# One pass of exponentials for both channel halves, those of one table parked in DRAM, together with a retuned queue scheduler

## The chip, the cores and the metric

The kernel runs on one core of one Trainium2 chip. The metric is the device time of one execution in microseconds (us), taken as the median of several executions. The profile is one execution of the same program; its span runs from the first instruction to the last and is some 1.8 us shorter than the time of that same execution.

Engines: TensorE (PE) multiplies matrices, VectorE (DVE) works element by element, ScalarE (ACT) evaluates functions and also copies results out of PSUM (the memory that matmuls write to), SyncE (SP) issues most transfers. GpSimd (POOL) does next to nothing (0.2 us). SBUF is the on-chip memory for everything else. The profile lists the clock that was granted to TensorE; a stretch is called warm here where it is near 1 and cold where it is near 0.5.

## The reference, cut to what matters

The output is a gate between two branches over 2048 positions and 512 channels:

```python
g = sigmoid((x * gate_w).sum(-1, keepdims=True))
return g * a + (1 - g) * b
# a: a state-space convolution, with 512 channels x 128 states
P = exp(logdA[:, :, None] * l)                    # complex, logdA = dt * (A_re + i A_im)
K = einsum("dn,dnl,dn->dl", Cc, P, dB).real       # one filter of 2048 taps per channel
y = irfft(rfft(u) * rfft(K)) + u * Dskip
# b: the two tokens of highest score go through a gated MLP (512 -> 1792 -> 512); below: the MoE
```

The kernel doesn't compute `P` for 2048 lags. It makes two small complex tables per half of the channels (table 1 with 32 lags, table 2 with 21), so that each needed lag is a product of one entry of each. A table entry is `exp(real part)` times the sine or cosine of the imaginary part. A matmul of table 1 with table 2 over the 128 states then gives the filter ("kernel generation"). The convolution is a blocked transform written as matmuls: forward transform of the input, spectrum of the filter, products in the frequency domain, inverse transform.

## The kernel before: the parts that matter

Every operation is recorded with what it reads and writes and with an estimated cost. A list scheduler then fixes the order of each engine's queue before the program is built. It takes, again and again, the operation that its model can start first; priority only decides between equal starts.

```python
class Prog:
    DMA_LAT, DMA_BW, SEM = 1.9, 200.0e3, 0.06
    ...
    def schedule(self):
        ...
                    if o.tset is not None and o.tset != phases[ph[0]]:
                        continue                     # table phases are strictly in order
                    e = e0
                    if o.alt is not None:            # ScalarE or VectorE, whichever the model has done first
                        e = min(o.alt, key=lambda x: max(free[x], rt[o.idx]) + o.alt[x][1] + self.bias.get(x, 0.0))
                    st = max(free[e], rt[o.idx])
                    key = (st, -o.bl - o.prio)
        ...
            free[e] = st + c
        ...
                rt[s] = max(rt[s], o.end + (self.SEM if ops[s].eng != e or o.dma else 0.0))
```

Two helpers may go to either engine, by their costs. `EV` copies a result out of PSUM, `SCL` multiplies by a constant:

```python
        def EV(o, a, rd, wr, **k):
            ...  cost=(0.185 + n * 0.833e-3, 0.16 + n * 1.04e-3)      # (ScalarE, VectorE)
        def SCL(o, a, c, rd, wr, **k):
            ...  cost=(0.2 + n * 0.833e-3, 0.18 + n * 0.55e-3)
```

The kernel has to load another set of function tables (ACT_TABLE_LOAD, 1.28 us in the traces) whenever ScalarE goes from `Exp` to `Sin` or back, so the two are separated into phases, `tset` 0 to 5. Even phases are exponentials, odd ones are everything else:

```python
        def exps1(h, ts):                            # table 1 of half h: 32 calls, 256 wide
            for s in range(32):
                AC(TP[h][1](0, 128, s * 4, (128, 64), (1, 4)), AL(0, 128, h * HC, (4, 64), (1, 4)), ACTF.Exp, ..., scale=float(T1[s]), tset=ts)
        def exps2(h, ts): ...                        # table 2: 16 calls, 256 wide
        exps1(0, 0); exps2(0, 0)
        P.boost = 100.0; routing(); P.boost = 0.0    # the MoE and the gate
        tab1(0, (1, 1)); forward(); tab2(0, (1, 3))
        exps1(1, 2); xupd(); kgen(0)
        ...
        tab1(1, (3, 3)); exps2(1, 4); tab2(1, (5, 5))
        kspec(0); kgen(1); products(0, 0); products(0, 1)
        ...
        kspec(1); inverse(0); products(1, 0); products(1, 1); inverse(1)
```

The reason for the phases of half 1 in the middle is memory. Nearly all of SBUF is taken by buffers that share places in turn. Table 2 of half 1 lies where the generated filter of half 0 lies for a while, and its exponentials lie where table 2 of half 0 was.

## Time and profile before

| | before |
|---|---|
| median of 4 executions | 225.21 us (224.63 to 226.58) |
| span of the profile | 225.8 us |
| busy PE, DVE, ACT | 182.8, 173.1, 151.0 us |
| table loads of ScalarE | 6 |

The first lines are of the page's part 1: busy time, share of the span, number of instructions.

```profile
## 1 busy us (share of the span) xinstructions
PE 182.8 (81%) x1480; PEld 111.4 (49%) x1490; DVE 173.1 (77%) x283; ACT 151.0 (67%) x282; POOL 0.2 (0%) x4
```

No engine is full. To see why they take turns, follow ScalarE and VectorE in the timeline. The columns are start, duration, engine, source line, operation, output and input with their shapes, count, and in brackets the idle time just before with what ended it. L398 is the helper of ScalarE functions, L402 the copy helper `EV`, L406 the scaling helper `SCL`, L387 VectorE's two-input operation, L391 its operation with a constant. First ScalarE:

```profile
28.25 1.28 ACT L242 ACT_TABLE_LOAD   x1
56.97 1.28 ACT L398 ACT_TABLE_LOAD   x1
70.93 3.46 ACT L398 ACTIVATE AR<-AR 128x256 bf16<-128x256 f32 x11
74.41 1.28 ACT L242 ACT_TABLE_LOAD   x1
108.39 1.28 ACT L398 ACT_TABLE_LOAD   x1
119.96 1.28 ACT L242 ACT_TABLE_LOAD   x1
```

Between 57 and 76 us and between 108 and 121 us, ScalarE makes half 1's exponentials and can compute no sine. VectorE, in its timeline, runs dry there:

```profile
59.46 0.78 DVE L387 TENSOR_TENSOR AR<-AR 128x28 bf16<-128x28 bf16 x2
73.13 0.68 DVE L396 CAST AR<-ps 2x512 bf16<-2x512 f32 x1 [12.89 <-PE ps L691]
76.69 1.23 DVE L402 CAST AR<-ps 128x1024 bf16<-128x1024 f32 x1 [2.50 <-PE ps L715]
116.71 0.69 DVE L402 CAST AR<-ps 128x512 bf16<-128x512 f32 x1 [4.35 <-PE ps L748]
122.34 0.69 DVE L391 TENSOR_SCALAR AR<-AR 128x1024 int32<-128x1024 int32 x1 [4.01 <-ACT AR L398]
146.08 64.98 DVE L387 TENSOR_TENSOR AR<-AR 128x1024 bf16<-128x1024 bf16 x74 [1.67 <-ACT AR L398]
```

The last line is the products of both halves, 65 us without a gap. So VectorE's time falls in three pieces: up to the products (146 us), the products (65 us), the tail with the last inverse (15 us). TensorE waits too, in its timeline, for an output scaling (L852, L853 are the matmuls of that step) that stands in ScalarE's queue behind half 1's new sines:

```profile
130.55 0.61 PE L852 MATMUL ps<-AR 128*128 128x512 bf16 x1 [10.19 <-ACT AR L398]
```

### The profile page before, as it was taken

The numbers are of one execution on the slowest core, as the hardware profiler recorded it, in microseconds if no ns is written. First come the engines' busy times: TensorE is split into PE (matmuls) and PEld (weight loads), VectorE is DVE, ScalarE is ACT, GpSimd is POOL, SyncE is SP. The second block draws the span as 40 slices with busy tenths as digits, with TensorE's granted clock in tenths as the row PEclk, the third lists the DMA queues.
The fourth block names the chain that finished last, engine by engine and source line by source line (L and its number), as shares of the span: only waits on it lengthen the run. The fifth ranks groups of instructions, "written<-read, shape, count | busy, mean of one in ns | idle before, by whom it ended". The sixth has DMA issues, their size and how long they took to land.

```text
span 225.8 us, 3655 instructions
## 1 busy us (share of the span) xinstructions
PE 182.8 (81%) x1480; PEld 111.4 (49%) x1490; DVE 173.1 (77%) x283; ACT 151.0 (67%) x282; POOL 0.2 (0%) x4
## 2 busy tenths in 40 slices
PE   0366798959999999997893089998898999945993
PEld 0255343626443444455650013666655768834882
DVE  0729369998600599999823999799999999999863
ACT  3799999998689896399969995656834455205000
POOL 0000000000000000000000000000000000000000
PEclk9999589967699999999667555999969999995899
DMA  6999940100902000000284000000090000002054
GB/s 95 363 312 319 405 192 1 36 13 3 302 23 49 0 0 0 0 3 1 79 381 193 0 1 0 3 0 0 3 345 29 0 3 0 0 0 73 23 162 117
DMA packets 17633, 19.93 MB, mean 88 GB/s; under 512 B 8913, under 2 KB 15186, under 8 KB 17234
## 3 DMA queue, kind: packets, MB, share of 16 engines
q1 hardware_dynamic: 16274, 19.48, 26.0%
q10 hardware_dynamic: 1344, 0.23, 0.9%
q8 instruction: 11, 0.18, 0.3%
q14 instruction: 4, 0.03, 0.0%
HBM read 16.83 MB, written 2.10 MB: 84 GB/s over the span
## 4 chain that ended last, share of the span: by engine, by line
PE 49%; DVE 23%; ACT 21%; issue 3%; DMA 2%; SPq 1%; DVEq 0%; ACTq 0%
DVE AR L387 19%; PE ps L715 18%; ACT AR L398 12%; PE ps L776 8%; PE ps L826 7%; ACT AR L402 6%; PE ps L735 3%; DVE AR L391 3%; PE ps L853 2%; ACT AR L406 2%; PE ps L852 2%; PE ps L748 2%; DMA AR<-in_A_A_im_dram 2%; PE ps L691 1%; PE ps L680 1%
## 5 line engine op out<-in xcount | busy, mean ns | idle before, releaser
L387 DVE TENSOR_TENSOR AR<-AR 128x1024 bf16<-128x1024 bf16 (+6 forms) x182 | 136.9, 804 | 9.3 <-DMA AR<-in_A_A_re_dram 5.8
L402 ACT ACTIVATE AR<-ps 128x1024 bf16<-128x1024 f32 (+7 forms) x62 | 50.2, 827 | 33.9 <-PE ps L776 17.3
L398 ACT ACTIVATE AR<-AR 128x256 bf16<-128x256 f32 (+4 forms) x132 | 65.1, 559 | 3.3 <-DVE AR L387 1.5
L715 PE MATMUL ps<-AR 128*128 128x512 bf16 x248 | 62.9, 408 | 2.0 <-ACT AR L402 1.1
L715 PEld LDWEIGHTS ps<-AR 128*128 128x128 bf16 x256 | 26.4, 104 | 35.5 <-issue 8.6
L826 PE MATMUL ps<-AR 128*128 128x256 bf16 x256 | 30.6, 285 | 5.5 <-ACT AR L398 5.5
L776 PE MATMUL ps<-AR 128*128 128x256 bf16 x224 | 32.9, 284 | 0.7 <-ACT AR L402 0.7
L826 PEld LDWEIGHTS ps<-AR 128*128 128x128 bf16 x256 | 26.1, 102 | 9.8 <-DVE AR L387 5.7
L776 PEld LDWEIGHTS ps<-AR 128*128 128x128 bf16 x224 | 21.7, 100 | 12.0 <-issue 1.5
L398 ACT ACTIVATE AR<-ps,AR 128x512 bf16<-128x512 f32 (+1 forms) x32 | 16.6, 584 | 15.5 <-DVE AR L387 10.3
L391 DVE TENSOR_SCALAR AR<-AR 128x1024 int32<-128x1024 int32 (+5 forms) x32 | 16.0, 523 | 4.7 <-ACT AR L398 4.3
L406 ACT ACTIVATE AR<-AR 128x256 int32<-128x256 f32 x50 | 17.2, 404 | 0.8 <-DVE AR L387 0.7
L607 PE MATMUL ps<-AR 128*128 128x128 bf16 x64 | 7.5, 311 | 11.6 <-DMA AR<-in_A_u_dram 9.5
L735 PE MATMUL ps<-AR 128*128 128x84 bf16 x256 | 13.3, 214 | 3.2 <-ACT AR L402 3.2
L852 PE MATMUL ps<-AR 128*128 128x512 bf16 x14 | 7.2, 512 | 10.2 <-ACT AR L398 10.2
L735 PEld LDWEIGHTS ps<-AR 128*128 128x128 bf16 x256 | 11.8, 106 | 5.1 <-ACT AR L402 4.3
L607 PEld LDWEIGHTS ps<-AR 128*128 128x128 bf16 x64 | 6.5, 145 | 12.4 <-DMA AR<-in_A_u_dram 9.5
L396 DVE CAST AR<-ps 128x16 bf16<-128x16 f32 (+3 forms) x6 | 1.5, 256 | 13.7 <-PE ps L691 12.9
L402 DVE CAST AR<-ps 128x1024 bf16<-128x1024 f32 (+4 forms) x7 | 5.7, 837 | 7.0 <-PE ps L748 4.4
L394 DVE SCALAR_TENSOR_TENSOR AR<-ps,AR 128x256 bf16<-128x256 f32 x16 | 6.9, 478 | 3.9 <-PE ps L826 3.9
L852 PEld LDWEIGHTS ps<-AR 128*128 128x128 bf16 x16 | 1.6, 99 | 15.0 <-ACT AR L398 13.1
L853 PE MATMUL ps<-AR 2*128 2x512 bf16 x16 | 7.9, 495 | 0.7 <-DVE AR L402 0.5
(35 smaller groups left out, 66.7 us busy)
## 6 DMA issues: line engine op xcount, KB each, us to landing
AR<-c_ksp SPq DMA_DIRECT2D x1, 3584.0 KB, 11.2
AR<-in_A_u_dram SPq DMA_DIRECT2D x2, 1024.0 KB, 7.2
AR<-c_fwd SPq DMA_DIRECT2D x1, 2048.0 KB, 7.9
AR<-c_inv SPq DMA_DIRECT2D x1, 2048.0 KB, 7.7
out_dram<-AR SPq DMA_DIRECT2D x16, 128.0 KB, 2.2
AR<-in_B_w_gate_dram SPq DMA_DIRECT2D x1, 1792.0 KB, 11.1
AR<-in_B_w_up_dram SPq DMA_DIRECT2D x1, 1792.0 KB, 12.6
AR<-in_B_w_down_dram SPq DMA_DIRECT2D x1, 1792.0 KB, 7.9
```

What stands on the lines that cost most here:

```text
L387: return P.op(DVE, lambda h: h.tensor_tensor(out=o, in0=a, in1=b, op=op), rd, wr, cost=tt_cost(o, a, b), **k)
L391: return P.op(DVE, lambda h: h.tensor_scalar(out=o, in0=a, scalar1=s1, scalar2=None, op0=op0), rd, wr, cost=c, **k)
L398: return P.op(ACT, lambda h: h.activation(out=o, in_=a, func=func, scale=scale, bias=bias), rd, wr, cost=0.185 + nel(o) * 0.833e-3 + (0.09 ...
L402: return P.op((ACT, DVE), (lambda h: h.activation(out=o, in_=a, func=ACTF.Copy), lambda h: h.tensor_copy(o, a)), rd, wr, cost=(0.185 + n * ...
L406: return P.op((ACT, DVE), (lambda h: h.activation(out=o, in_=a, func=ACTF.Copy, scale=c), lambda h: h.tensor_scalar(out=o, in0=a, scalar1= ...
L607: last = h.transpose(bb(0, 128, db * 256 + t_ * 128, (1, 128)), U(0, 128, (2 * q + t_) * D + db * 128, (1, 128)), IDN(0, (1, 128)))
L715: last = h.matmul(o, w, U(0, 128, (blk * 8 + st * 2 + par) * D, (1, D)), start=(par + st == 0), stop=(par * 4 + st == 7 and blk == 0))
L735: last = hh.matmul(pb(0, 128, (g - b0) * 84, (1, 84)), TP[h][1 - part](0, 128, g * 128, (1, 128)), TQ[h][1 - part](0, 128, g * 84, (1, 84) ...
L776: last = hh.matmul(pb(0, 128, n * 256, (1, 256)), KP(0, np_, u * 2048 + tau * 128, (1, 128)), KC[h](0, np_, jg * 256, (1, 256)), start=(k ...
L826: last = hh.matmul(pb(0, 128, e * 256, (1, 256)), G(0, 128, ((par * 2 + part) * 4 + ft) * 512 + (2 * t2 + e) * 128, (1, 128)), X(0, 128, h ...
L852: h.matmul(pb(0, 128, c0, (1, D)), IDN(0, (1, 128)), U(0, 128, tb * D, (1, D)), start=True, stop=False)
L853: return h.matmul(pb(0, 128, c0, (1, D)), OHR(0, 2, tb * 128, (1, 128)), ZB(0, 2, D, (1, D)), start=False, stop=True)
```

## The change

Its stated intent: all exponentials of both halves come first, in one pass that is 512 wide, with one switch of tables. Half 1's table 2 exponentials are written to DRAM and read back when their place is free. To make room for half 1's table 1 exponentials, one MoE weight moves to the space of the input spectrum, so the forward transform now does all of block 0 before block 1. The diff also retunes the scheduler's costs and adds priorities ("boosts"). Two smaller edits are left out of the cut: the sign changes of the sine table, fixed on VectorE before, may now go to either engine (`SCL`), and the two parts of each forward group are separate operations. Its core, cut:

```diff
-    DMA_LAT, DMA_BW, SEM = 1.9, 200.0e3, 0.06
+    DMA_LAT, DMA_BW, SEM, OVER = 1.9, 300.0e3, 0.08, 0.085
-            free[e] = st + c
+            free[e] = st + c - (self.OVER if e in (ACT, DVE) and not o.dma else 0.0)
-                rt[s] = max(rt[s], o.end + (self.SEM if ops[s].eng != e or o.dma else 0.0))
+                rt[s] = max(rt[s], o.end + (self.SEM if ops[s].eng != e or o.dma else 0.03))
 # EV, the copy out of PSUM: (ScalarE, VectorE)
-                        cost=(0.185 + n * 0.833e-3, 0.16 + n * 1.04e-3), **k)
+                        cost=(0.185 + n * 0.833e-3, 0.16 + n * (1.04e-3 if a.dtype == F32 else 0.52e-3)), **k)
 # SCL
-                        cost=(0.2 + n * 0.833e-3, 0.18 + n * 0.55e-3), **k)
+                        cost=(0.19 + n * 0.833e-3, 0.165 + n * (0.48e-3 if a.dtype == F32 else 0.245e-3)), **k)
 ...                                               # and the costs of two VectorE helpers and of small matmuls
+        PK = Buf(P, "park", AR[:, :], "dram", 0, 4, BF)
+        park = nc.dram_tensor("park", (128, 4 * KB), BF).ap()
-        def exps1(h, ts):
+        def exps1(ts):
             for s in range(32):
-                AC(TP[h][1](...), AL(0, 128, h * HC, (4, 64), (1, 4)), ACTF.Exp, ...)
+                AC(two(TP[0][1], TP[1][1], s * 4, 128), AL(0, 128, 0, (HC, 2), (4, 64), (1, 4)), ACTF.Exp, ...)
 ...                                               # exps2 likewise: half 0 in place, half 1 into ST
-            for ft in range(4):
-                for blk in range(NBLK):            # forward
+            for blk in range(NBLK):
+                for ft in range(4):
-        exps1(0, 0)
-        exps2(0, 0)
+        exps1(0)
+        exps2(0)
+        DMA([(... park ..., ST(0, 128, 0, (1, 4 * KB)))], [ST], [PK], 1048576)
-        tab2(0, (1, 3))
-        exps1(1, 2)
+        P.boost = 30.0
+        tab2(0, (1, 1))
+        P.boost = -30.0
+        tab1(1, (1, 1))
+        P.boost = 0.0
         xupd()
+        P.boost = 60.0
         kgen(0)
-        tab1(1, (3, 3))
-        exps2(1, 4)
-        tab2(1, (5, 5))
+        DMA([(B("eb1b", oE, 8 * KB)(...), ... park ...)], [PK], [...], 1048576)
+        tab2(1, (1, 1))
```

## The prediction

> **What bounds it now.** No engine binds alone: busy are TensorE 182.8, VectorE 173.1, ScalarE 151.0 of 225.8 us. The chain of waits runs over TensorE (49%), VectorE (23%) and ScalarE (21%) in turn. The timeline shows three parts.
> - Up to 146 us, VectorE builds the tables of both halves. It is idle here for about 43 us: 5.8 at the start, 4.6 (25 to 30 us), 12.9 (60 to 73) and 2.5, 4.4 and 4.0 (112 to 122), the rest small.
> - From 146 to 211 us, it does the spectral products without a gap.
> - The last inverse and the output follow, about 15 us.
>
> The idle stretches at 60 to 78 and 112 to 122 are ScalarE's doing: the Sin of later tables must wait until half 1's exponentials (57 to 74, 108 to 120) are done, with a table switch on either side. TensorE waits 10.2 us there too, at 120 us, for an output scaling that stands in ScalarE's queue behind new Sin work; its matmuls then run cold (granted clock 0.54 from 120 to 139 us; 512 wide spaced 0.54 us instead of 0.22).
>
> **What it removes.** 96 exponentials 256 wide become 48 that are 512 wide. In a queue, 26 of the former took 7.94 us, 0.305 each, 29 us in all; the latter are an estimated 0.52 each, 25 us. Six table loads of 1.28 us become two. ScalarE saves about 9 us. More important, no exponential phase lies in the middle, so Sin, scalings and evictions may come in any order, and half 1's first table can fill the wait for half 0's kernel generation. The Trainium skill ("ScalarE: Activation LUTs", What ACT_TABLE_LOAD costs) gives 1283 ns for the load, as the trace, and about as much for a drain, which the trace does not show.
>
> **What it adds.** The first exponential phase grows by about 48 x 0.21 = 10 us, and with it the switch (28.2 us now) moves to about 37 to 40. Forward matmuls, routing and copies fill part of that on TensorE and VectorE. Parking writes and reads 1 MB each; from 2 MB landing in 7.7 us I estimate 4 to 6 us each. The write is off the path; the read waits for kernel generation 0 and is mostly hidden by its selection step. Six more small weight loads in the forward (5.7 us to landing, against about 7 us of matmuls each) should hide. MoE weights in spectrum space delay only the second block. The retuned scheduler costs reorder all queues: not separable in advance.
>
> **Critical path.** VectorE from 30 to 146 us has about 88 us of work. Starting it 10 us later, with routing and some copies done before, and 6 to 8 us of idle, tables end at an estimated 125 to 131. The products (65) and the tail (15) follow unchanged: 205 to 211. From TensorE: forward starts at 24 us, about 168 us of matmuls at the warm spacing and a tail of 4 give 196 without a stall, and 8 to 10 us of stalls are likely. Both meet near 207.
>
> **Predicted:** 207 us, 198 to 217 (8 in 10). Faster 0.93, same 0.05, slower 0.02.
>
> **What the profile would show.** Two table loads; 48 exponentials of about 0.62 us busy; the switch at 37 to 40 us; no VectorE gap over 6 us after 40 us; the 10.2 us TensorE wait gone and the clock there above 0.8; products starting at 125 to 133; busy sums of VectorE and TensorE within 5% of before.
>
> **What would make it wrong.** The late switch starving VectorE and TensorE for over 10 us; the parked read landing behind the 3.5 MB load (11.2 us); the small weight loads stalling the forward; half 0's kernel generation queued late behind the forward; a colder TensorE.

## The result, and the profile after

The changed kernel took 212.8 us (211.06 to 213.95, 4 executions), the kernel before in the same rounds 225.21 us. The ratio is 0.943 with a 95% interval of 0.936 to 0.951. A ratio here is the mean time of one kernel's runs over that of the other's runs of the same rounds, so it is not quite the ratio of the medians. Executions over 1.5% slower than the fastest of the same kernel are left out of the means. Later the same kernel gave 212.64 us and 0.940 (0.935 to 0.945): repeats agree to about 0.3%.

The lines that answer to those of before are of the same views. Part 1 of the page, then ScalarE and the group of exponentials, before and after (in the view of groups by shape, "25.4, 621" is busy us and mean ns of one):

```profile
## 1 busy us (share of the span) xinstructions
PE 180.4 (85%) x1490; PEld 109.8 (52%) x1490; DVE 173.8 (82%) x292; ACT 138.1 (65%) x221; POOL 0.2 (0%) x4
```

```profile
17.50 16.21 ACT L398 ACTIVATE AR<-AR 128x512 bf16<-128x512 f32 x31
33.73 1.28 ACT L242 ACT_TABLE_LOAD   x1
```

```profile
L398 ACT ACTIVATE AR<-AR 128x256 bf16<-128x256 f32 x96 | 31.0, 405 | 1.5 <-DVE AR L387 1.5
L398 ACT ACTIVATE AR<-AR 128x512 bf16<-128x512 f32 x48 | 25.4, 621 | 1.2 <-DVE AR L387 1.2
```

ScalarE saves 13 us of work. VectorE and TensorE have the same work as before. VectorE's timeline after the switch has no long hole; these are its largest ones up to the last product:

```profile
98.05 0.90 DVE L406 TENSOR_SCALAR AR<-AR 128x256 int32<-128x256 f32 x4 [1.12 <-ACT AR L398]
103.90 1.29 DVE L387 TENSOR_TENSOR AR<-AR 128x1024 bf16<-128x1024 bf16 x2 [4.95 <-DMA AR<-park]
108.20 3.10 DVE L387 TENSOR_TENSOR AR<-AR 128x1024 bf16<-128x1024 bf16 x5 [3.01 <-PE ps L773]
124.79 35.73 DVE L387 TENSOR_TENSOR AR<-AR 128x2048 bf16<-128x2048 bf16 x48 [1.82 <-ACT AR L402]
162.09 9.43 DVE L387 TENSOR_TENSOR AR<-AR 128x2048 bf16<-128x2048 bf16 x10 [1.56 <-ACT AR L402]
173.28 21.19 DVE L387 TENSOR_TENSOR AR<-AR 128x1024 bf16<-128x1024 bf16 x26 [1.76 <-ACT AR L398]
```

TensorE's wait of 10.19 us for the output scaling (its matmuls are L871 and L872 here) is gone; the longest waits there now are these:

```profile
112.63 0.39 PE L871 MATMUL ps<-AR 128*128 128x512 bf16 x1 [0.63 <-ACT AR L398]
114.15 0.61 PE L871 MATMUL ps<-AR 128*128 128x512 bf16 x1 [0.65 <-ACT AR L398]
```

Divide the two spans as VectorE's timeline divides them:

| VectorE's pieces, us | before | after | difference |
|---|---|---|---|
| up to the first product | 146.1 | 124.8 | -21.3 |
| products | 65.0 | 69.7 | +4.7 |
| after the last product | 14.7 | 16.7 | +2.0 |
| span | 225.8 | 211.2 | -14.6 |

The front became 21 us shorter, and 6.7 us of that were given back later. The product piece holds 84 VectorE instructions where it held 75: some of the last table operations of half 1 now stand among the first products, and there are two waits in it, of 1.56 and 1.76 us. So the products begin earlier than the tables end.

### The profile page after: what moved, and what is told of

Its sections match the earlier page's. It is cut to its first block, busy times and chain, and to the rows that moved or that the text cites. A ratio compares the mean times of both kernels' runs of the same rounds, so it can differ in the third digit from the quotient of the medians.

```text
span 211.2 us, 3613 instructions
## 1 busy us (share of the span) xinstructions
PE 180.4 (85%) x1490; PEld 109.8 (52%) x1490; DVE 173.8 (82%) x292; ACT 138.1 (65%) x221; POOL 0.2 (0%) x4
## 4 chain that ended last, share of the span: by engine, by line
DVE 40%; PE 32%; ACT 22%; DMA 3%; SPq 1%; issue 1%; DVEq 0%
DVE AR L387 33%; ACT AR L398 15%; PE ps L845 9%; PE ps L795 8%; ACT AR L402 5%; PE ps L767 4%; PE ps L754 3%; DVE AR L391 3%; DMA AR<-in_A_u_dram 3%; PE ps L623 2%; PE ps L734 2%; PE ps L872 1%; PE ps L871 1%; DVE AR L402 1%; DVE AR L406 1%; SPq L483 1%
## 5 line engine op out<-in xcount | busy, mean ns | idle before, releaser
L387 DVE TENSOR_TENSOR AR<-AR 128x1024 bf16<-128x1024 bf16 (+6 forms) x182 | 134.6, 798 | 19.2 <-DMA AR<-in_A_A_re_dram 5.2
L402 ACT ACTIVATE AR<-ps 128x1024 bf16<-128x1024 f32 (+7 forms) x59 | 45.5, 787 | 34.0 <-PE ps L795 19.9
L398 ACT ACTIVATE AR<-AR 128x512 bf16<-128x512 f32 (+3 forms) x84 | 59.3, 770 | 5.2 <-DVE AR L391 3.7
L734 PEld LDWEIGHTS ps<-AR 128*128 128x128 bf16 x256 | 25.6, 102 | 31.6 <-issue 5.9
L845 PEld LDWEIGHTS ps<-AR 128*128 128x128 bf16 x256 | 25.5, 101 | 9.1 <-DVE AR L387 5.2
L795 PEld LDWEIGHTS ps<-AR 128*128 128x128 bf16 x224 | 22.2, 101 | 13.6 <-ACT AR L402 2.6
L406 ACT ACTIVATE AR<-AR 128x256 int32<-128x256 f32 (+1 forms) x44 | 19.1, 492 | 0.2
L754 PEld LDWEIGHTS ps<-AR 128*128 128x128 bf16 x256 | 12.6, 110 | 7.7 <-ACT AR L402 3.7
L623 PE MATMUL ps<-AR 128*128 128x128 bf16 x64 | 6.4, 278 | 9.9 <-DMA AR<-in_A_u_dram 9.4
L391 DVE TENSOR_SCALAR AR<-AR 128x1024 int32<-128x1024 int32 (+4 forms) x24 | 13.2, 550 | 0.3
L623 PEld LDWEIGHTS ps<-AR 128*128 128x128 bf16 x64 | 5.4, 127 | 10.8 <-DMA AR<-in_A_u_dram 9.4
L406 DVE TENSOR_SCALAR AR<-AR 128x256 int32<-128x256 f32 (+1 forms) x28 | 7.0, 292 | 2.8 <-ACT AR L398 2.7
L767 PE MATMUL ps<-AR 128*32 128x128 bf16 (+1 forms) x96 | 8.4, 381 | 0.7 <-ACT AR L402 0.7
L402 DVE CAST AR<-ps 128x1024 bf16<-128x1024 f32 (+1 forms) x6 | 6.7, 1124 | 2.1 <-PE ps L734 2.1
L871 PE MATMUL ps<-AR 128*128 128x512 bf16 x16 | 7.3, 455 | 1.3 <-ACT AR L398 1.3
L872 PE MATMUL ps<-AR 2*128 2x512 bf16 x16 | 7.4, 465 | 0.0
```

The source lines that it names most:

```text
L387: return P.op(DVE, lambda h: h.tensor_tensor(out=o, in0=a, in1=b, op=op), rd, wr, cost=tt_cost(o, a, b), **k)
L391: return P.op(DVE, lambda h: h.tensor_scalar(out=o, in0=a, scalar1=s1, scalar2=None, op0=op0), rd, wr, cost=c, **k)
L398: return P.op(ACT, lambda h: h.activation(out=o, in_=a, func=func, scale=scale, bias=bias), rd, wr, cost=0.185 + nel(o) * 0.833e-3 + (0.09 ...
L402: return P.op((ACT, DVE), (lambda h: h.activation(out=o, in_=a, func=ACTF.Copy), lambda h: h.tensor_copy(o, a)), rd, wr, cost=(0.185 + n * ...
L406: return P.op((ACT, DVE), (lambda h: h.activation(out=o, in_=a, func=ACTF.Copy, scale=c), lambda h: h.tensor_scalar(out=o, in0=a, scalar1= ...
L623: last = h.transpose(bb(0, 128, db * 256 + t_ * 128, (1, 128)), U(0, 128, (2 * q + t_) * D + db * 128, (1, 128)), IDN(0, (1, 128)))
```

## The experiments

Twelve kernels ran. All passed the comparison with the reference, even `tiny_reload`, which reads wrong data; for that one it only says that the error stays within the tolerance. In the table, "switch" is the start of the load that ends the first exponentials, and the span is that of the profile.

| kernel | median us (lowest to highest) | ratio to before (95%) | switch | span |
|---|---|---|---|---|
| before (first comparison) | 225.21 (224.63 to 226.58) | 1 | 28.25 | 225.8 |
| changed (first comparison) | 212.8 (211.06 to 213.95) | 0.943 (0.936 to 0.951) | 33.73 | 211.2 |
| three_phases | 221.52 (220.84 to 223.63) | 0.983 (0.977 to 0.989) | 25.03 | 220.0 |
| costs_alone | 219.34 (219.02 to 220.22) | 0.972 (0.968 to 0.977) | 25.83 | 217.4 |
| exp_256 | 215.71 (214.6 to 216.63) | 0.956 (0.952 to 0.960) | 37.99 | 214.9 |
| tiny_reload | 212.58 (210.6 to 213.83) | 0.940 (0.935 to 0.945) | 33.80 | 211.1 |
| extra_loads | 217.1 (215.11 to 218.69) | 0.959 (0.954 to 0.965) | 35.55 | 215.4 |
| old_costs | 224.3 (223.37 to 224.37) | 0.992 (0.986 to 0.999) | 38.00 | 222.5 |
| forward_first | 211.4 (210.28 to 212.66) | 0.936 (0.931 to 0.941) | 33.73 | 209.4 |
| tables_first | 213.43 (212.6 to 214.71) | 0.946 (0.941 to 0.951) | 35.36 | 212.5 |
| after_again | 212.64 (211.17 to 213.66) | 0.940 (0.935 to 0.945) | 34.47 | 211.9 |
| old_copy_costs | 216.37 (215.74 to 217.92) | 0.959 (0.954 to 0.964) | 42.53 | 214.0 |
| old_forward | 215.4 (214.35 to 216.01) | 0.952 (0.947 to 0.958) | 34.04 | 212.6 |
| first_and_late | 211.42 (210.76 to 212.72) | 0.935 (0.931 to 0.940) | 34.21 | 209.2 |

The kernel before was run again, on another chip each time: 226.35, 225.85 and 226.31 us. So kernels are best compared by their ratios. The highest run of `tiny_reload` and of `extra_loads` is a slow one; without it their medians are 212.32 and 216.95 us.

One caution for the last two columns. They are of one execution each, and in some executions the input lands late: TensorE's first transpose started at 9.4 us in the profiles of before, changed, exp_256, tiny_reload, forward_first and others, at up to 10.2 us, and at 11.1 to 11.3 us in those of extra_loads, old_costs and tables_first.

### Is it the pass, or the scheduler's costs?

Theory A, the prediction's, was that the gain comes from taking the exponential phases out of the middle. The rival, theory B, was that it comes from the retuned costs. `three_phases` takes the pass alone away. It needs one more order, between two copies of one PSUM bank that landed on different engines:

```diff
-        def exps1(ts):
+        def exps1(h, ts):
-                AC(two(TP[0][1], TP[1][1], s * 4, 128), ...)
+                AC(TP[h][1](0, 128, s * 4, (128, 64), (1, 4)), AL(0, 128, h * HC, (4, 64), (1, 4)), ACTF.Exp, ...)
-        tab2(0, (1, 1))
+        tab2(0, (1, 3)); exps1(1, 2)
-        tab1(1, (1, 1))
+        tab1(1, (3, 3))
-        DMA(... park read ...); tab2(1, (1, 1))
+        exps2(1, 4); tab2(1, (5, 5))
-    EV(KC[h](0, 32, 1280, (1, 256)), ..., [pb.buf], [(KC[h], 3)])
+    EV(KC[h](0, 32, 1280, (1, 256)), ..., [pb.buf, (KC[h], 2)], [(KC[h], 3)])
```

> The changed kernel with half 1's exponentials put back into phases of their own (256 wide, six table loads, no parking); all the rest of the change (retuned scheduler costs, forward order, boosts) stays. Theory A, the one of the prediction: the gain comes from taking the exponential phases out of the middle; then this is near the kernel before, 220 to 227 us, and VectorE is idle again for over 10 us around the phase of the first tables. Theory B: the gain comes from the retuned costs and the new order of queues; then this stays at 211 to 216 us.

`costs_alone` is the kernel before with all lines of the diff that only change costs (the lines on `DMA_BW`, `SEM`, `OVER`, `EV`, `SCL` above, those of two VectorE helpers and the small matmuls'), and nothing else.

> The kernel before with nothing but the retuned costs of the scheduler. Theory A: 222 to 227 us, as before. Theory B: 211 to 217 us, most of the gain without touching one exponential.

`old_costs` is the other corner: the changed kernel with those cost lines put back, and the same added order between the two copies.

> The changed kernel with the scheduler costs of before (and one added order between two copies of the same PSUM bank, which the check demands). The costs alone gave 7 us on the kernel before. If their gain and that of the single exponential pass add up, this is at 218 to 221 us; if they overlap, at 213 to 216.

Two by two, as ratios to the kernel before:

| | old costs | new costs |
|---|---|---|
| exponentials in three phases | 1 (before) | 0.972 (costs_alone); 0.983 with the new forward and boosts (three_phases) |
| one pass | 0.992 (old_costs) | 0.943 and 0.940 (changed) |

Neither theory stands as stated. `three_phases` met theory A's number, but `costs_alone` met neither: 219.34 us lies between the two. The pass is worth 0.8% at the old costs (forward order and boosts included) and 3 to 4% at the new ones, depending on which of the two kernels it is held against. The new costs are worth 2.8% without the pass and about 5% with it. The two add up to 3.6%, and together they give 5.7 to 6.0%: each makes room for the other. No run takes the boosts alone away. The expectation of 218 to 221 us for `old_costs`, had the gains added up, was missed on the upper side.

The traces show what the pass takes away. In `three_phases` VectorE's worst wait, in the timeline, is this one:

```profile
93.79 0.29 DVE L406 TENSOR_SCALAR AR<-AR 128x256 int32<-128x256 f32 x1 [1.62 <-ACT AR L398]
94.00 1.22 DVE L387 TENSOR_TENSOR AR<-AR 128x2048 bf16<-128x2048 bf16 x1
109.80 0.41 DVE L402 CAST AR<-ps 32x256 bf16<-32x256 f32 x1 [14.58 <-ACT AR L402]
```

Here is ScalarE at the same time in `three_phases`, with the exponential phase between the two loads:

```profile
102.03 1.28 ACT L398 ACT_TABLE_LOAD   x1
103.32 1.95 ACT L398 ACTIVATE AR<-AR 128x256 bf16<-128x256 f32 x6
111.58 1.28 ACT L242 ACT_TABLE_LOAD   x1
```

The releaser named, ScalarE's copy, is the one that this kernel's added order makes VectorE wait for, so the 14.58 us are partly made by the experiment: the matmuls that this copy needs ended at 108.4 us, so 1.4 us of them at most. VectorE's next table work came only at 113.96 us, after another wait of 1.63 us for the first sine behind the phase. Nor is so long a wait a mark of every kernel with phases in the middle: in `costs_alone` the longest after the switch are 6.39 and 5.53 us. How much of the 2.2 us between `three_phases` and `costs_alone` is due to the added order, and how much to the forward order, the boosts and the freed sign changes, was not separated.

And `old_costs` shows why the pass alone brings so little. The one pass is there, the switch is at 38.0 us as the prediction had it, but VectorE keeps waiting for ScalarE's sines and scalings. These are a few of its waits in the timeline:

```profile
96.20 0.69 DVE L391 TENSOR_SCALAR AR<-AR 128x1024 int32<-128x1024 int32 x1 [2.37 <-ACT AR L398]
105.75 0.50 DVE L406 TENSOR_SCALAR AR<-AR 128x256 int32<-128x256 f32 x2 [1.82 <-ACT AR L398]
111.91 0.29 DVE L406 TENSOR_SCALAR AR<-AR 128x256 int32<-128x256 f32 x1 [2.29 <-ACT AR L398]
143.64 64.98 DVE L387 TENSOR_TENSOR AR<-AR 128x1024 bf16<-128x1024 bf16 x74 [1.87 <-ACT AR L398]
```

From its switch to its products `old_costs` takes 105.6 us, with VectorE busy 84.5; the changed kernel takes 91.1 us with 78.2 busy. That is 21.1 against 12.9 us of idle, with less work left in the stretch besides. The same count gives 29.8 us of idle for the kernel before, 27.6 for `three_phases` and 20.6 for `costs_alone`. So the pass alone does take 8.7 us of idle away, but its switch comes 9.75 us later than before (1.8 of them by late input), and that eats most of it. The Trainium skill ("Perfetto Trace Analysis", Tensor Engine Instruction (MATMUL, LD_WEIGHTS)) says that ScalarE's and VectorE's queues are strictly first in, first out; the trace of before agrees, in that the results of output matmuls that had ended by 120.4 us were scaled only from 129.8 us on, behind the sines that stood before them in ScalarE's queue. The better order alone (2.8%) was worth more than the pass alone (0.8%).

### Which of the costs?

`old_copy_costs` puts only the costs of `EV` and `SCL` back.

```diff
-  cost=(0.185 + n * 0.833e-3, 0.16 + n * (1.04e-3 if a.dtype == F32 else 0.52e-3))
+  cost=(0.185 + n * 0.833e-3, 0.16 + n * 1.04e-3)
-  cost=(0.19 + n * 0.833e-3, 0.165 + n * (0.48e-3 if a.dtype == F32 else 0.245e-3))
+  cost=(0.2 + n * 0.833e-3, 0.18 + n * 0.55e-3)
```

> The changed kernel with the old scheduler costs of the copies and scalings alone (1.22 us for a VectorE copy of 1024 bf16 out of PSUM, which takes 0.69 in the traces). If these two costs carry the gain of the retuning (the whole of it was 11.5 us on the changed kernel), more of the transposes' copies go to ScalarE, the switch moves about 3 us later and the time rises to 218 us or more. If the overlap term and the wait costs carry it, it stays below 216.

It took 216.37 us against 212.64 in the same rounds, 3.7 us more: between the two expectations. The Trainium skill ("VectorE: DVE Perf Modes", Why PSUM operands drop a tier) says that a PSUM operand in fp32 leaves VectorE at its basic rate, and that for any other at most the doubled rate is to be had. The trace agrees: a copy of 1024 elements out of PSUM took 690 ns in bf16 and 1217 ns in fp32. The old cost line gave both 1.22 us. So the model sent the transposed inputs, which are bf16, to ScalarE. In the view of groups by shape, first the changed kernel, then `old_copy_costs`:

```profile
L402 DVE COPY AR<-ps 128x1024 bf16<-128x1024 bf16 x6 | 4.1, 690 | 1.2 <-PE ps L623 1.2
L402 DVE CAST AR<-ps 128x1024 bf16<-128x1024 f32 x5 | 6.1, 1217 | 2.1 <-PE ps L734 2.1
L402 ACT ACTIVATE AR<-ps 128x1024 bf16<-128x1024 bf16 x2 | 2.0, 1018 | 0.3 <-PE ps L623 0.3
```

```profile
L402 ACT ACTIVATE AR<-ps 128x1024 bf16<-128x1024 bf16 x8 | 7.5, 1036 | 0.8 <-PE ps L623 0.8
```

Six of the eight copies are on VectorE in the changed kernel, none in `old_copy_costs`. That is one reason why the switch came at 33.7 us. In `old_copy_costs` it came at 42.5 us, yet only 3.7 us of those 8.8 reached the end: the stretch after the switch was 171.5 us there against 177.5. That difference was not taken apart. The rest of the new costs' worth, some 8 us of 11.7 (224.3 less 212.64), lies with the overlap term, the wait costs, the transfer rate, the two VectorE helpers and the small matmuls; which of them was not separated.

### Width of the exponentials and the loads themselves

`exp_256` issues each 512 wide exponential as two 256 wide ones, with the queue orders unchanged.

```diff
+            def two_halves(h):
+                for i in range(2):
+                    oo = bass.AP(o.tensor, o.offset + i * o.ap[1][0], [o.ap[0]] + list(o.ap[2:]))
+                    aa = bass.AP(a.tensor, a.offset + i * a.ap[1][0], [a.ap[0]] + list(a.ap[2:]))
+                    r = h.activation(out=oo, in_=aa, func=ACTF.Exp, scale=scale, bias=0.0)
+                return r
```

> The changed kernel, queue orders unchanged, but each exponential 512 wide is issued as two 256 wide ones. ScalarE then needs about 48 x 0.09 = 4.3 us more before the table switch. If VectorE and TensorE really wait for the switch (theory A's cost of the change), the switch moves from 33.7 to about 38 us and the time rises by 3 to 5 us, to 215 to 218. If the front has slack, the rise is under 1.5 us.

The switch moved from 33.7 to 38.0 us and the time rose by 2.9 to 3.1 us (215.71 less 212.8 or 212.64). That is within what was expected: the switch is on the critical path, and about 70% of its delay reaches the end. In the trace the delay is still whole when the parked read is issued (104.37 us instead of 99.06). Then 1.6 us of it are made up, because the forward group between kernel generation and selection runs warm here (8 matmuls in 1.73 us) and cold in the profile of the changed kernel (3.43 us). The Trainium skill ("ScalarE: Activation LUTs", What ACT_TABLE_LOAD costs) gives 0.833 ns per element, a fixed cost of 186 ns, and an overlap of about 93 ns between neighbours. From these figures an estimated 93 ns is saved for each call that is not made. The traces agree: 26 calls in a row took 7.94 us before, 0.305 each, and 31 of the wide ones 16.10 us after, 0.519 each; two narrow ones less a wide one is 0.091 us.

`extra_loads` puts four table loads back into ScalarE's queue, in two pairs, with no exponentials.

```diff
+            if o.tag == "switch":
+                h.preload_act_table_set("exp_and_others")
+                h.preload_act_table_set("silu_and_others")
...
-            AC(so(0), lo, ACTF.Sin, ks, [(s, "s")], scale=SC16, tset=ts)
+            AC(so(0), lo, ACTF.Sin, ks, [(s, "s")], scale=SC16, tset=ts, tag="switch" if na[0] in (7, 15) else "")
```

> The changed kernel, queue orders unchanged, with two round trips of table loads (four loads of 1.28 us) put back into ScalarE's queue, one before the third Sin group of each half's second table. If the loads themselves were a large part of the cost of the phases, the time rises by 4 to 5 us. If it was the place of the phases and the waits that they force, and not the loads, it rises by less than 2 us.

It took 217.1 us, or 216.95 without its one slow run. Against the changed kernel that is 4.2 to 4.3 us more. The two were not in the same rounds; the ratios to before, 0.959 against 0.940 and 0.943, say 3.6 to 4.3 us. The loads came as intended (source lines are shifted by three in this kernel):

```profile
55.25 1.33 ACT L409 ACTIVATE AR<-AR 128x256 int32<-128x256 f32 x4
56.60 1.28 ACT L240 ACT_TABLE_LOAD   x1
57.89 1.28 ACT L241 ACT_TABLE_LOAD   x1
59.18 1.06 ACT L401 ACTIVATE AR<-AR 128x1024 bf16<-128x1024 int16 x1
```

So the four loads, 5.1 us of ScalarE, cost most of their length, and theory's "less than 2 us" was wrong. The trace shows it for each pair. After the first, ScalarE is nearly full (58.7 us busy of 62.7 between 36.3 and 99 us in the changed kernel), and the parked read is issued 67.0 us after the switch instead of 65.3, 1.7 us late. After the second, VectorE waits 1.91 and 0.72 us for ScalarE where the changed kernel has no such waits. Yet from the switch to the end only 2.4 us were lost in this execution (179.9 us against 177.5): between the two pairs, the forward group that ran cold in the profile of the changed kernel (3.43 us) ran warm here (1.73 us). A further 1.8 us were lost before the switch, where TensorE started 2 us late, which has nothing to do with the loads. How the 4.2 us of the times divide between loads and late input is therefore not settled. Up to half of what `three_phases` loses to the changed kernel, 8.7 us, can thus be the loads alone.

### The parked read and the 8 us hole

The largest holes left, 4.95 and 3.01 us, lie at 99 to 108 us. The first is put down to the read of the parked data. `tiny_reload` reads 8 KB instead of 1 MB, with the queue orders unchanged.

```diff
-        DMA([(B("eb1b", oE, 8 * KB)(0, 128, 0, (1, 4 * KB)), bass.AP(park.tensor, 0, [[4 * KB, 128], [1, 4 * KB]]))], [PK],
+        DMA([(B("eb1b", oE, 8 * KB)(0, 1, 0, (1, 4 * KB)), bass.AP(park.tensor, 0, [[4 * KB, 1], [1, 4 * KB]]))], [PK],
```

> Wrong result on purpose: the read back of the parked exponentials fetches 8 KB instead of 1 MB, queue orders unchanged. The changed kernel's VectorE waits 4.95 us for this read at 99 us and 3.0 us for the selection matmuls at 105 us. If the read is what costs, the time falls by 2 to 4 us. If the selection step, whose input lies where table 1 is to be written, is what holds table 1, the first wait shrinks, the second grows by as much, and the time changes by less than 1 us.

The time did not change: 212.58 us. The same two lines of VectorE's timeline in `tiny_reload`:

```profile
103.45 1.29 DVE L387 TENSOR_TENSOR AR<-AR 128x1024 bf16<-128x1024 bf16 x2 [4.42 <-PE ps L736]
108.29 3.10 DVE L387 TENSOR_TENSOR AR<-AR 128x1024 bf16<-128x1024 bf16 x5 [3.54 <-PE ps L773]
```

The wait is now put down to the last forward matmul (L736), and the second wait has grown by what the first lost. This is the general trap of such lines: the name in the bracket is the last of several releasers, and one that came 0.5 us earlier is hidden behind it. Table 2 of half 1 lies over the small forward weights and over the generated filter of half 0, so it waits for the end of the forward, for the selection matmuls (L773) and for the read. (The texts here call it "table 1".)

`forward_first` lets the last two groups of kernel generation come after all of the forward.

```diff
-                P.op(PE, mm, [*TP[h], *TQ[h]], [pb.buf], cost=ng * 2 * 0.05)
+                ko = P.op(PE, mm, [*TP[h], *TQ[h]], [pb.buf], cost=ng * 2 * 0.05)
+                if h == 0 and b0 >= 54:
+                    ko.deps.update(P.fws)          # all forward operations
```

> The changed kernel with one more order: the last two matmul groups of kernel generation 0 come after all forward matmuls. In the changed kernel one forward group runs cold (3.5 us) between kernel generation and selection, and table 1 waits for both. If that order is what makes the 8 us idle of VectorE at 99 to 108 us, the idle falls by 2 to 3.5 us and the time by 1 to 3 us. If kernel generation itself is late for VectorE, nothing is gained (within 1 us of the changed kernel).

It took 211.4 us, 1.2 to 1.4 us less than the changed kernel, at the lower end of what was expected, and the intervals of the ratios overlap. But the hole did not close: VectorE still waits 1.12, 2.24, 4.29 (for the parked read) and 0.59 us between 96 and 108 us. The forward group now runs warm (1.9 instead of 3.5 us), kernel generation ends later in exchange, and the read, which starts when it ends, lands at 106 us. But the new order isn't shown to be what made it warm: with the old one the same group ran warm in the profiles of `exp_256`, `extra_loads` and `tables_first` (8 matmuls in 1.73 us) and cold in those of the changed kernel, `after_again` and `tiny_reload` (3.43 us). So the gain of about 1.3 us may be the clock's. All three engines are nearly full in the stretch before: in the changed kernel TensorE was busy for 60.6, VectorE for 60.2 and ScalarE for 58.7 of the 62.7 us.

### Order of products, inverse and forward

`tables_first` lets half 0's products begin only when half 1's tables are done.

```diff
-                TT(v4(PA), xv(blk), kv(0, 0), MUL, kx(blk) + kk(0, 0), [PA])
+                TT(v4(PA), xv(blk), kv(0, 0), MUL, kx(blk) + kk(0, 0) + (list(TQ[1]) if (h, qd, blk) == (0, 0, 1) else []), [PA])
```

> The changed kernel with one more order: the products of half 0 start only when half 1's tables are done. In the changed kernel, some 9 us of products lie among the last table operations, so kernel generation 1 starts at 142 us and VectorE later waits 1.6 us for its spectrum. If that interleaving costs time, kernel generation 1 starts at about 134 us and the time falls by 1 to 3 us; if VectorE's sum of work is all that counts, it stays within 1 us.

It took 213.43 us, no gain. Kernel generation 1 starts at 140.7 us instead of 142.1 (134 was expected, but TensorE is busy with half 0's spectrum until then), the products start at 129.6 instead of 124.8. The mixing of tables and products therefore costs nothing of note: VectorE does the same work in another order. The earlier start of the products in the table of VectorE's pieces is partly a matter of that order.

`first_and_late` is `forward_first` with half 0's inverse after all of half 1's spectrum.

```diff
-    P.op(PE, iv, [G] + [xk(h, blk, part, par, ft) for ...], ...)
+    P.op(PE, iv, [G] + ([KK[1]] if h == 0 else []) + [xk(h, blk, part, par, ft) for ...], ...)
```

> forward_first with one order more: the inverse of half 0 comes after all of kernel spectrum 1, as in the kernel before (in the changed kernel six inverse groups of half 0 lie among it, and VectorE waits 1.76 us at 171.5 us for a scaled output of the first). If these waits count, 208 to 210 us, under forward_first's 211.4; if VectorE's sum of work counts, 211 to 212.

It took 211.42 us, as `forward_first` did; the waits only moved (1.90 us at 159.5 and 2.57 us at 176.8 us). These two are the fastest kernels, with ratios of 0.936 and 0.935. `first_and_late` ran in the same rounds as the changed kernel, and its interval (0.931 to 0.940) overlaps that one's (0.935 to 0.945). So "1.2 us faster" is likely and not proven.

`old_forward` is the changed kernel with the forward in its old order; the edit also makes the two parts of each forward group one operation again, which the cut leaves out.

```diff
-            for blk in range(NBLK):
-                for ft in range(4):
+            for ft in range(4):
+                for blk in range(NBLK):
```

> The changed kernel with the forward in its old order (both blocks of one frequency tile together, two instead of six later weight loads). The weights of the MoE now lie where block 1 of the spectrum goes, so the old order should make TensorE wait for the MoE matmuls at about 30 to 40 us. If the new order is needed for the single pass, the time rises by 2 to 6 us; if it is a matter of taste, it stays within 1.5 us.

It took 215.4 us, 2.8 us more, in the expected range but not for the expected reason alone. TensorE's wait at the MoE (before 48.4 us) is only 2.5 us. The larger sign in its trace is VectorE's wait for the parked read, 10.27 us instead of 4.95. The read is no slower (4.8 us to landing in both), it starts later: the last matmuls of kernel generation begin at 104.92 us instead of 98.55, and the read is issued at 105.43 instead of 99.06. What in the order delays kernel generation was not followed further.

> The changed kernel itself, unedited, as the reference of this call: 211 to 214 us, ratio about 0.943. Differences between the runs of this call are read against this one.

`after_again` is the unedited changed kernel. It gave what was expected.

## Why the prediction was right or wrong, point by point

The time, 212.8 us, lies in the predicted range of 198 to 217 and 5.8 us above the centre of 207.

- **What bounds the kernel before**: right as far as it goes: bringing the phases back costs 8.7 us (`three_phases`), or 6.5 if the changed kernel is held against `costs_alone`, and VectorE's waits are there again. It left out that the order around the phases was poor too: `costs_alone` gains 2.8% with all phases in place.
- **The pass saves ScalarE about 9 us and delays the switch by 10 us**: right for the calls themselves, 0.519 us each against the estimate of 0.52. ScalarE's busy sum fell by 13 us, not 9: 5.6 by the exponentials, 5.1 by the loads, and 4.7 by copies that moved to VectorE (ScalarE's copies out of PSUM took 50.2 us before and 45.5 after). Its scalings grew from 17.2 to 19.1 us, as six of the eight freed sign changes went to it, at 1.04 us each where VectorE had taken 0.42. The switch came at 33.7 us, not 37 to 40. At the old costs it came at 38.0 us (with 1.9 us of late input); the new copy cost, which the prediction did not use, left two of the eight copies on ScalarE, where `old_copy_costs` put all eight there and the kernel before five.
- **"The retuned scheduler costs reorder all queues: not separable in advance"**: this is the step that failed, although the total came out right. Having called them not separable, the prediction gave them no share and laid the whole gain on the pass. On the chip the pass alone at the old costs is worth 0.8%, the costs alone 2.8%, both 5.7 to 6.0%. `old_costs` is the case that the prediction had worked out: there the switch came at 38.0 us as forecast, but VectorE was then idle for 21.1 us and not for 6 to 8, and the products started at 143.6 us and not at 125 to 131. The pass does little by itself: it allows a better order, and the old costs did not find it.
- **"Tables end at an estimated 125 to 131. The products (65) and the tail (15) follow unchanged"**: the products started at 124.8 us, but that was partly luck: the switch came 3 to 6 us earlier than forecast, and the idle time after it was 5 to 7 us longer. Products and tail took 86.4 us, not 80. The product piece took 69.7 us, with 1.9 us more work in it (66.1 against 64.2 busy) and two waits; the tail took 16.7 us. This is the term that was mis-sized. By `tables_first`, the early start and the longer product piece are two sides of one order. A further 1.8 us of the miss is that the estimate was made in spans of the profile, which are that much below the times.
- **"6 to 8 us of idle"**: too low. From the switch to the first product VectorE was idle for 12.9 us (91.07 us with 78.20 of work). 8 us of it is the hole at 99 to 108 us, which no experiment closed.
- **The parked read**: right. It landed in 4.8 us (4 to 6 was the estimate) and costs nothing by `tiny_reload`. The parked write took 14.9 us to land, not 4 to 6, next to the MoE weights, and nobody waited for it.
- **TensorE's wait of 10.2 us gone**: right. **The clock there above 0.8**: wrong. From 114.1 to 119.5 us the output scaling still ran at a granted clock of 0.50, 0.54 us per matmul. The Trainium skill ("TensorE: Matmul & The Clock Gate", What's actually happening) says that an idle window of about 3.4 us throttles the clock, and that a busy one of that length releases it. The trace of before agrees with the first half: after the wait of 10.19 us the clock was 0.50. It does not show the second: from 130.5 to 139.1 us the output matmuls followed each other without a gap, 8.6 us long, and the clock stayed at 0.50; it rose only while the matmuls of the spectrum ran that came next. In the changed kernel only short waits preceded (0.63 and 0.65 us in the timeline), so no run shows which rule took the clock down. The prediction's 0.22 us is the warm spacing of the forward; the output step's own is 0.32.

## What to carry to other kernels

Where a scheduler fixes each queue's order, its cost table is part of the kernel: check each cost line against the durations in the trace first, since a copy priced at 1.22 us that takes 0.69 goes to the wrong engine. Test a change that mixes a structural part with retuned costs two by two; here one part alone gave hardly anything and the other about half of the whole. And before mending a wait, shrink the releaser that the trace names: if the time stays and another name takes its place, several releasers end together.

## What the Trainium skill lacked or had wrong

- "ScalarE: Activation LUTs", What ACT_TABLE_LOAD costs, adds a drain of about 1.38 us to each load of 1.283 us. No trace here shows one: in `extra_loads` the first load starts 0.02 us after the scalings before it end, the second 1.29 us after the first, and the next sine 1.29 us after that.
- "TensorE: Matmul & The Clock Gate" gives 215.7 and 426.7 ns between matmuls 512 wide, warm and cold. The forward agrees (8 in 1.73 us warm, 0.216 each; 8 in 3.43 us cold, 0.429 each). The output step, which alternates between weights of 128 and of 2 rows, took 0.32 us warm and 0.54 us cold per matmul in all traces. The trace of before shows where the rest goes: each weight load of 0.10 us starts there with its own matmul, while in the forward it starts some 0.2 us before (65.50 against 65.71 us), during the matmul ahead of it. No page that was read names this alternation, and no run shows why the load is not moved ahead.
- Which matmuls count as busy for the clock: no page that was read says it for such a pattern. The output step alone did not bring the clock back in 8.6 us (0.50 from 130.5 to 139.1 us, before).
